# Attention and rational feed-forward on one core: output tiles take a buffer of another tag, and the transposed softmax weights are moved directly behind the transpose

## The chip, the cores and the metric

The kernel runs on one core of a Trainium2 chip, in one launch. The metric is the device time of an execution in microseconds (us). A core has several engines that each work through a queue of their own, in order, and that wait for each other by semaphores: PE (TensorE, matmuls; the loads of its stationary operand are listed as PEld), DVE (VectorE, elementwise work and reductions), ACT (ScalarE, functions and copies), POOL (GpSimd) and SP (SyncE), which here does nothing but issue transfers (DMA). Matmuls write to PSUM, whose banks are handed out to tiles like any other buffer; other tiles lie in SBUF.

## The reference

Chunked attention over 8 batches, 8 heads, 576 rows and 64 columns a head, in chunks of 64 rows, and behind it a feed-forward layer whose activation is a rational function.

```python
def _attn_ref(q, k, v):
    ...
    scores = scale * np.matmul(q_c, k_c.transpose(0, 1, 2, 4, 3))
    scores = scores - np.max(scores, axis=-1, keepdims=True)
    attn = np.exp(scores)
    attn = attn / (np.sum(attn, axis=-1, keepdims=True) + 1e-09)
    out = np.matmul(attn, v_c)
    return out.reshape(B, H, S, D).astype(np.float32)

def _moe_ref(x, w_in, w_out, a, b):
    h = x @ w_in
    h2 = h * h
    h3 = h2 * h
    P = a[0] + a[1] * h + a[2] * h2 + a[3] * h3
    Q = 1.0 + np.abs(b[0]) * np.abs(h) + np.abs(b[1]) * h2
    g = P / (Q + 1e-06)
    return (g @ w_out).astype(np.float32)

def reference(**kwargs):
    ...
    attn_out = _attn_ref(**attn_kwargs)
    B, H, S, D = attn_out.shape
    x = np.ascontiguousarray(attn_out.transpose(0, 2, 1, 3)).reshape(B * S, H * D)
    return _moe_ref(x=x, **moe_kwargs)
```

x has 4608 rows and 512 columns, `w_in` is 512x2048, `w_out` 2048x512.

## The kernel before

The 4608 rows are worked through in 18 blocks n of 256 rows (`NB`, `BT`). Each matmul of the feed-forward is done with operands split into a high and a low part (`xhi`, `xlo`, `wi_hi`, `wi_lo`, `ghi`, `glo` and so on), as three products: high by high, low by high, high by low. A block's hidden layer is cut into four steps s of 512 columns (`NST`), so a block is four steps; step g in the list `steps` is block and quarter. In a step

- `ff1` (tokens F and f, L374) makes `ph`, 48 products into a pair of PSUM banks p0 or p1, in turn from step to step;
- the chain (a, b, c, Q, I, p, J, P, g, H, R, G) makes `ghi` and `glo` of it: ACT does L378 to L398, DVE L390 to L424, with `glo` on POOL in some steps;
- `ff2` (Z, z, y, L583) adds the step two before, `LAG`, into `po`.

Beside this runs the attention of later blocks, spread over the steps. For block m = n + 1: its softmax sums and the division (n, Np) in step 0; `att_turn` (T) in step 1, a transpose on DVE within 32x32 squares, from `e` into `et` (L315); `att_move` (K), also in step 1, which sets the squares in their places by 16 transfers from `et` to `at`, issued by SP one after the other (L323); `att_av` (A) in step 3, 64 small products `psx` of `at` and `v` (L214), and behind it X and Y, which make `xhi` (ACT, L353) and `xlo` (DVE, L357), read by all `ff1` of the next block. Block n + 2 has its scores `pss`, maxima and exponentials `e` in step 3. Behind `att_av` and the scores SP loads v, q and k of the block after.

The last step of blocks 5 to 16 is not added by `ff2` but by a scheme with seven products of half size (`ff2_seven`, L540): `s_hi` and `s_lo` make `shi` and `slo` in step 0 of the next block (h, l), the products run in step 1 (V) into `xacc` and `po`, and `s_store` (w, L549 to L553) and `s_out` (o, L558) put the output tile `o` together on ACT and DVE; `put` stores it by four transfers (L600). The other blocks have `store` (L594), a copy of `po` on ACT and the same four transfers; in blocks from 3 on, it stands where V, w and o stand.

What each engine does in which order is written out by hand: `START` for the opening part up to step 12, the first of block 3, and `STEADY`, one line of tokens for each of a block's four steps, for the rest. Within an engine the order of the tokens is the order of its queue. Waits follow from the tiles: a tile is a buffer of its tag, each tag has two (`p2`) if nothing else is said, and whoever takes a buffer over waits until the last reader of the tile before is done. The tags that matter: `eo` holds `e`, `et`, `at`, `o` and, in blocks 3 and 4, `tsum`; `xhi` holds `xhi` and `shi`. In a block before the change, `eo` is given to `et` (T), then to `o` in the place of `e` (w), then to `at` in the place of `o` (K).

Of the kernel before, what the change touches and what calls it, by code (L numbers as in the profile page):

```python
# [10 lines left out]
F32 = mybir.dt.float32  # L11
# [8 lines left out]
P = 128  # L20
# [5 lines left out]
DM = 512  # L26
# [31 lines left out]
def tile_chunked_attention_rational_moe(  # L58
# [13 lines left out]
    p2 = ctx.enter_context(tc.tile_pool(name="p2", bufs=2))  # L72
# [359 lines left out]
    sums, tw, shi, slo, xacc, wide = {}, {}, {}, {}, {}, {}  # L432
# [110 lines left out]

    def s_store(n):
        x, po = xacc.pop(n), obuf.pop(n)
        wide[n] = o = p2.tile([P, 2, DM], F32, tag="eo", name=f"o{n}")
        flat = o.rearrange("p a b -> p (a b)")
        block = lambda i, k=1: flat[:, 256 * i:256 * (i + k)]
        nc.scalar.copy(block(0), x[:, 0, 0:256])  # L549
        nc.vector.tensor_add(block(1), block(0), x[:, 0, 256:512])  # L550
        nc.vector.tensor_add(block(2), block(1), x[:, 1, 0:256])
        nc.vector.tensor_add(block(3), block(2), x[:, 1, 256:512])
        nc.vector.tensor_add(block(1), block(1), x[:, 1, 256:512])  # L553
        obuf["late", n] = po
# [35 lines left out]
        return out[n * BT:(n + 1) * BT, :].rearrange("(u c t) f -> c u t f", u=UPB, c=2)  # L590

    def store(n):
        o = p2.tile([P, 2, DM], F32, tag="eo", name=f"o{n}")
        nc.scalar.copy(o, obuf.pop(n))  # L594
        put(n, o)

    def put(n, o):
        for c in range(2):
            for u in range(UPB):
                nc.sync.dma_start(out=rows_out(n)[c, u], in_=o[64 * u:64 * u + 64, c, :])  # L600
# [42 lines left out]
    def qk(n, u=None):  # L643
# [10 lines left out]
        "S": att_s, "M": att_max, "U": att_sub, "E": att_exp, "n": att_rs, "N": att_norm,  # L654
        "T": att_t, "K": att_copy, "A": att_av, "X": att_xhi, "Y": att_xlo,
        "O": store,
    }
    for k, letter in enumerate("Ff"):
# [10 lines left out]
    def run(program, then=""):  # L669
# [14 lines left out]
    one = lambda names, k: run(" ".join(f"{x}{k}" for x in names.split()))  # L684
    STEADY = (
# [4 lines left out]
    )  # L690
# [1 line left out]
    def step(g):  # L692
# [8 lines left out]
        of_early = {"S": lambda k: (att_s(k), load_qk(k + 1)), "M": att_max, "U": att_sub,  # L701
                    "E0": lambda k: att_exp_half(k, 0), "E1": lambda k: att_exp_half(k, 1)}
        of_prev = {"s": s_sums, "h": s_hi, "l": s_lo, "lp": lambda k: s_lo(k, nc.gpsimd), "w": s_store, "o": s_out}
        other = {"Q": chain_nq, "I": chain_nln, "g": chain_t, "H": chain_inv, "R": chain_g, "G": chain_split, "Gp": chain_split}
        tokens = STEADY[s].split()
        for token in tokens:
# [17 lines left out]
            elif name in of_prev:  # L724
                if fast:
                    of_prev[name](n - 1)
            elif name == "V":
                if fast:
                    ff2_seven(n - 1)
                    run(f"y{g - LAG - 1}", "F")  # L730
                else:
                    run(" ".join(f"{x}{g - LAG}" for x in "Zzy"), "F")
                    store(n - 1)
            elif name in "Zzy":
                if not (s == 0 and fast and name == "y"):
                    last = "z" if s == 0 and fast else "y"
                    run(f"{name}{g - LAG}", "F" if name == last else "z")
            elif late and s == 0 and fast and name in other:
                other[name](*steps[k])
            elif late and s == 0 and fast and name in ("L", "Lp"):  # L740
                chain_rest(*steps[k], nc.gpsimd if name == "Lp" else None)
            elif name in ("L", "Lp"):
                pass
            elif not late and s == 3 and whole and name in other:
                other[name](*steps[k])
            elif late and g == FIRST:
                pass
            elif name == "Gp" and (g == FIRST or n == NB - 1):
                run(f"G{g}")
            else:  # L750
                run(f"{name}{k}")
# [45 lines left out]
```

## Time and profile before

| | |
|---|---|
| Time, median of 3 runs | 881.47 us (879.83 to 885.39) |
| The profiled execution: its own time | 880.04 us |
| Its span, from first to last instruction | 878.2 us |
| Around the span | 1.84 us |
| Granted clock of PE, mean over the span | 0.997 |
| Moved by the transfers | 63.26 MB, mean 72 GB/s |

The page and the other views are of that one profiled execution. Busy time counts the instructions of an engine, not its waits; an instruction's row gives its start, its length in us and, in brackets, the idle time before it with what ended it. A matmul's end is modelled, and matmuls overlap: each is listed as longer than the distance to the next. `L374 PE MATMUL ph<-xhi,wi_hi` means line 374, engine PE, from `xhi` and `wi_hi` into `ph`. SPq is the queue of SP, whose instructions issue transfers. Blocks 3 to 17, the part in the order of `STEADY`, take three quarters of the span.

### The profile page before, as it was taken

What the parts mean: (1) busy time and instruction counts of PE and PEld (TensorE: products, weight loads), DVE (VectorE), ACT (ScalarE), POOL (GpSimd) and SP (SyncE); (2) the same over time, 40 slices, a digit from 0 to 9 for tenths busy, and PEclk for the clock granted to TensorE, in tenths of its full rate; (3) what the DMA queues carried; (4) which work ended last, traced back from release to release, by engine and by line L of the source; (5) the groups of instructions that cost most, each with busy time, mean ns of one, the idle gap of its engine ahead of it and who ended that gap; (6) DMA issues with size and microseconds to landing.
All of it is one profiled execution on the core that took longest, in us unless ns stands there. A gap on an engine that the chain in (4) does not pass through costs nothing.

```text
span 878.2 us, 21405 instructions
## 1 busy us (share of the span) xinstructions
PE 850.5 (97%) x9200; PEld 836.9 (95%) x9200; DVE 766.2 (87%) x753; ACT 564.3 (64%) x958; POOL 134.2 (15%) x64
## 2 busy tenths in 40 slices
PE   5999999999999999999999999999999999999998
PEld 3899999999999999999999999999999999999997
DVE  6999998997888888889899898989888888898886
ACT  5999865755647665658574757575666657584553
POOL 1222222001313111110201111111111111102000
PEclk9999999999999999999999999999999999999999
DMA  8653204012121203030211212121212030201010
GB/s 317 258 217 138 104 25 145 26 43 80 34 89 26 97 18 103 2 90 33 52 70 49 73 44 80 37 85 32 92 25 97 14 108 2 73 2 49 1 25 25
DMA packets 27263, 63.26 MB, mean 72 GB/s; under 512 B 6176, under 2 KB 13344, under 8 KB 25120
## 3 DMA queue, kind: packets, MB, share of 16 engines
q1 hardware_dynamic: 27008, 61.63, 21.8%
q8 instruction: 72, 1.18, 0.5%
q10 hardware_dynamic: 160, 0.26, 0.1%
q14 instruction: 23, 0.19, 0.1%
HBM read 45.09 MB, written 9.44 MB: 62 GB/s over the span
## 4 chain that ended last, share of the span: by engine, by line
PE 62%; SPq 18%; DMA 9%; DVE 5%; ACT 3%; issue 3%; DVEq 0%; ACTq 0%
PE ph L374 24%; PE po L583 24%; SPq L323 15%; PE xacc L540 4%; DMA out<-o 4%; DMA at<-et 3%; PE po L540 3%; SPq L600 3%; PE psx L214 2%; PE pss L214 2%; DVE o L558 2%; DMA raw<-in_w_in 1%; ACT e L298 1%; DMA v<-in_vP 1%; PE pe L583 1%
## 5 line engine op out<-in xcount | busy, mean ns | idle before, releaser
L374 PE MATMUL ph<-xhi,wi_hi 128*128 128x256 f32 x1152 | 320.8, 278 | 0.3 <-ACT xhi L353 0.3
L374 PE MATMUL ph<-xlo,wi_hi 128*128 128x256 f32 x1152 | 319.1, 277 | 1.2 <-DVE xlo L357 0.9
L374 PE MATMUL ph<-xhi,wi_lo 128*128 128x256 f32 x1152 | 318.8, 277 | 0.0
L374 PEld LDWEIGHTS ph<-xlo,wi_hi 128*128 128x128 f32 x1152 | 216.8, 188 | 1.2 <-DVE xlo L357 1.1
L374 PEld LDWEIGHTS ph<-xhi,wi_hi 128*128 128x128 f32 x1152 | 216.2, 188 | 1.6 <-ACT xhi L353 0.9
L374 PEld LDWEIGHTS ph<-xhi,wi_lo 128*128 128x128 f32 x1152 | 216.5, 188 | 0.3 <-issue 0.3
L583 PE MATMUL po<-wo_hi,ghi 128*128 128x256 f32 (+2 forms) x920 | 182.7, 280 | 0.0
L583 PE MATMUL po<-wo_lo,ghi 128*128 128x256 f32 (+2 forms) x920 | 180.9, 278 | 0.0
L424 POOL TENSOR_TENSOR glo<-B,A 128x1024 fp32r<-128x1024 f32 x36 | 88.7, 2465 | 437.7 <-DVE B L419 325.0
L394 ACT ACTIVATE A<-B,cst 128x1024 f32<-128x1024 f32 x60 | 69.4, 1156 | 121.8 <-DVE B L390 116.7
L583 PEld LDWEIGHTS po<-wo_hi,ghi 128*128 128x128 f32 x920 | 139.8, 189 | 0.9
L583 PEld LDWEIGHTS po<-wo_lo,ghi 128*128 128x128 f32 x920 | 139.8, 189 | 0.0
L378 ACT ACTIVATE A<-ph,ab 128x1024 f32<-128x1024 f32 x72 | 81.7, 1135 | 82.9 <-PE ph L374 79.6
L583 PE MATMUL po<-wo_hi,glo 128*128 128x256 f32 (+2 forms) x920 | 115.2, 277 | 0.0
L583 PEld LDWEIGHTS po<-wo_hi,glo 128*128 128x128 f32 x920 | 109.4, 188 | 0.2
L406 DVE SCALAR_TENSOR_TENSOR C<-C,ab,ph 128x1024 f32<-128x1024 f32 x72 | 92.2, 1281 | 3.1 <-ACT B L382 0.7
L386 ACT ACTIVATE C<-ph,ab 128x1024 f32<-128x1024 f32 x72 | 88.5, 1230 | 10.0 <-PE ph L374 10.0
L390 DVE SCALAR_TENSOR_TENSOR B<-B,ab,A 128x1024 f32<-128x1024 f32 x60 | 82.2, 1371 | 10.4 <-POOL glo L424 5.3
L402 DVE TENSOR_TENSOR C<-C,ph 128x1024 f32<-128x1024 f32 x72 | 86.7, 1204 | 0.4 <-ACT A L378 0.3
L398 ACT ACTIVATE A<-A,cst 128x1024 f32<-128x1024 f32 x72 | 83.1, 1155 | 2.2
L411 DVE SCALAR_TENSOR_TENSOR ghi<-C,ab,A 128x1024 fp32r<-128x1024 f32 x60 | 77.0, 1284 | 8.4 <-ACT A L398 2.0
L419 DVE SCALAR_TENSOR_TENSOR B<-C,ab,B 128x1024 f32<-128x1024 f32 x60 | 77.1, 1284 | 1.9
(140 smaller groups left out, 1150.2 us busy)
## 6 DMA issues: line engine op xcount, KB each, us to landing
v<-in_vP SPq DMA_DIRECT2D x18, 512.0 KB, 4.2
out<-o SPq DMA_DIRECT2D x68, 128.0 KB, 2.4
raw<-in_w_in SPq DMA_DIRECT2D x8, 1024.0 KB, 6.3
raw<-in_w_out SPq DMA_DIRECT2D x8, 1024.0 KB, 4.9
qk<-in_qT SPq DMA_DIRECT2D x16, 512.0 KB, 5.2
qk<-in_kT SPq DMA_DIRECT2D x16, 512.0 KB, 6.0
at<-et SPq DMA_DIRECT2D x224, 32.0 KB, 1.9
Aqk<-in_qT SPq DMA_DIRECT2D x2, 256.0 KB, 4.5
```

The lines of the kernel that those rows point to most:

```text
L323: nc.sync.dma_start(out=at[32 * j:32 * j + 32, i, :, :], in_=t[32 * i:32 * i + 32, j, :, :])
L374: nc.tensor.matmul(ph[:, fi, :], w[:, cc, f], x[:, cc, :], start=(k == 0), stop=(k == len(mm) - 1))
L378: nc.scalar.activation(ch[n, s][1], ch[n, s][0], AF.Abs, scale=b0)
L386: nc.scalar.activation(ch[n, s][3], ch[n, s][0], AF.Identity, bias=a2, scale=a3)
L390: nc.vector.scalar_tensor_tensor(B, B, b1a, A, ALU.mult, ALU.add)
L398: nc.scalar.activation(A, A, AF.Exp, bias=cst[:, 1:2], scale=-1.0)
L402: nc.vector.tensor_mul(C, C, h)
L406: nc.vector.scalar_tensor_tensor(C, C, a1, h, ALU.add, ALU.mult)
L411: nc.vector.scalar_tensor_tensor(gbuf[n, s][0], C, a0, A, ALU.add, ALU.mult)
L419: nc.vector.scalar_tensor_tensor(B, C, a0, B, ALU.add, ALU.subtract)
L424: (engine or nc.vector).tensor_mul(gbuf[n, s][1], B, A)
L583: nc.tensor.matmul(accs[n][i][:, cols], g[:, fi, i * 128:(i + 1) * 128], w[:, FPS * s + fi, cols], start=start, stop=stop,)
```

## The change

Three things. The output tile of `s_store` takes a buffer of the tag `xhi` instead of `eo`; so does that of `store` for blocks from 2 on. And in step 1, the token K stands directly behind T, ahead of V, w and o, where it stood behind these.

```diff
     def s_store(n):
         x, po = xacc.pop(n), obuf.pop(n)
-        wide[n] = o = p2.tile([P, 2, DM], F32, tag="eo", name=f"o{n}")
+        wide[n] = o = p2.tile([P, 2, DM], F32, tag="xhi", name=f"o{n}")
...
     def store(n):
-        o = p2.tile([P, 2, DM], F32, tag="eo", name=f"o{n}")
+        o = p2.tile([P, 2, DM], F32, tag="xhi" if n > 1 else "eo", name=f"o{n}")
         nc.scalar.copy(o, obuf.pop(n))
         put(n, o)
...
-        "F f a b c T V w o K Q I p J P g H R G",
+        "F f a b c T K V w o Q I p J P g H R G",
```

With it `eo` is given to `et` (T) and to `at` in the place of `e` (K); `o` takes, of the two buffers of `xhi`, the one that holds no live `xhi`: in the blocks with seven products that of `shi`, and the next block's `xhi` then follows `o` in it.

The order on SP, steps 1 to 3 of three blocks, before; numbers behind the names are those of the tiles.

```order
L600 DMA out<-o_3377 64x512 x4
L323 DMA at_3383<-et_3327 32x256 x16
L123 DMA v_3608<-in_vP 128x1024
L117 DMA qk<-in_qT 128x1024
L117 DMA qk<-in_kT 128x1024
L600 DMA out<-o_3960 64x512 x4
L323 DMA at_3971<-et_3899 32x256 x16
L123 DMA v_4196<-in_vP 128x1024
```

The same place of SP's queue after the change:

```order
L323 DMA at_3329<-et_3327 32x256 x16
L600 DMA out<-o_3394 64x512 x4
L123 DMA v_3608<-in_vP 128x1024
L117 DMA qk<-in_qT 128x1024
L117 DMA qk<-in_kT 128x1024
L323 DMA at_3901<-et_3899 32x256 x16
L600 DMA out<-o_3977 64x512 x4
L123 DMA v_4196<-in_vP 128x1024
```

The 16 transfers of `at` have changed places with the four stores of `o`; nothing else moved on SP. On the other engines no instruction changes its place. What they wait for does change; on ACT, the first copy into `o` in step 1, with the semaphores that it waits for (those of the DMA queues begin with DMAHW):

```order
 L382 ACTIVATE B_1_3895<-ph_1_3844 128x1024
 L386 ACTIVATE C_1_3897<-ph_1_3844,ab 128x1024
-L549 COPY o_3960<-xacc_3901 128x256 [waits DVE_49,PE_49]
+L549 COPY o_3977<-xacc_3918 128x256 [waits PE_49]
 L394 ACTIVATE A_1_3893<-B_1_3895,cst 128x1024 [waits DVE_49,Activation_49]
 L398 ACTIVATE A_1_3893<-A_1_3893,cst 128x1024 [waits Activation_49]
```

The copy no longer waits for DVE, whose transpose read the buffer's last tile `e`. In step 3 of the same block, again on ACT, the cast into `xhi`:

```order
 L382 ACTIVATE B_3_4235<-ph_3_4114 128x1024
-L353 CAST xhi_4237<-psx_4163 128x2x4x128 [waits PE_49]
+L353 CAST xhi_4237<-psx_4163 128x2x4x128 [waits DMAHW4_49,DMAHW3_49,DMAHW5_49,DMAHW2_49,PE_49]
 L386 ACTIVATE C_3_4241<-ph_3_4114,ab 128x1024
 L478 ACTIVATE A_3_4233<-B_3_4235,cst 128x1024 [waits DVE_49,Activation_49]
```

The cast, in its old place, now also waits for four transfers, the stores of `o`.

## The prediction

> **What bounds the kernel now.** I read the page first, then the waits of PE, then the order of time around one of these waits on PE, SP, DVE and ACT.
>
> The page: busy time of each engine and its share of the span.
> ```profile
> span 878.2 us, 21405 instructions
> PE 850.5 (97%) x9200; PEld 836.9 (95%) x9200; DVE 766.2 (87%) x753; ACT 564.3 (64%) x958; POOL 134.2 (15%) x64
> ```
> PE is the bound, so only what PE idles through, or runs at a lower clock, can be won. The waits of PE and of its weight loads from 180 to 820 us (engine, line, releaser: total, times, longest) are these alone:
> ```profile
> PE psx L214 <- DMA at<-et: 11.8, 17, 1.2
> PEld psx L214 <- issue: 8.9, 12, 1.3
> PEld psx L214 <- DMA at<-et: 4.9, 6, 0.9
> ```
> In the steady part PE waits for one thing: the moved softmax weights `at`, which the products `psx` read. SP's own waits hold the row that says why `at` is late: the 16 transfers of L323 stand behind the four output stores in SP's queue, and must also wait until those have landed, because `at` takes the buffer of `o`.
> ```profile
> SPq L323 <- DMA out<-o: 24.0, 27, 1.8
> ```
> One block in order of time (start, length, what, idle before it), first DVE and ACT, then SP, then PE; here `et` is the transposed tile, `o` the output tile:
> ```profile
> 367.82 1.24 DVE L315 STREAM_TRANSPOSE et<-e 128x1024 f32<-128x1024 f32 x1
> 369.14 0.37 ACT L549 COPY o<-xacc 128x256 f32<-128x256 f32 x1 [0.78 <-DVE et L315]
> 371.81 1.22 DVE L558 TENSOR_TENSOR o<-o,po 128x1024 f32<-128x1024 f32 x1 [0.60 <-PE po L583]
> 384.27 1.28 DVE L406 SCALAR_TENSOR_TENSOR C<-C,ab,ph 128x1024 f32<-128x1024 f32 x1
> 389.23 1.02 ACT L382 ACTIVATE B<-ph 128x1024 f32<-128x1024 f32 x1
> 390.94 1.01 ACT L353 CAST xhi<-psx 128x1024 fp32r<-128x1024 f32 x1 [0.69 <-PE psx L214]
> 391.99 1.23 DVE L357 TENSOR_TENSOR xlo<-psx,xhi 128x1024 fp32r<-128x1024 f32 x1 [2.43 <-ACT xhi L353]
> ```
> ```profile
> 373.10 2.43 SPq L600 DMA_DIRECT2D out<-o  x4
> 377.44 10.75 SPq L323 DMA_DIRECT2D at<-et  x16
> ```
> ```profile
> 388.12 0.45 PE L214 MATMUL psx<-at,v 64*64 64x64 f32 x6
> 389.79 1.05 PE L214 MATMUL psx<-at,v 64*64 64x64 f32 x57 [1.23 <-DMA at<-et]
> 390.69 0.22 PE L214 MATMUL psx<-at,v 64*64 64x64 f32 x1
> ```
> `et` is ready at 369.06, but its first transfer goes out at 377.44, 8.4 us later; the issue of 16 takes 10.75 us and the last lands about when PE is already in `psx`. PE can start `psx` at 388.12 and ends at 390.91.
>
> **The change part by part.** *The move of K ahead of V, w and o, and the new buffer of `at`.* Nothing is added or removed: the same 16 transfers and 4 stores, in the other order, on SP. After it the transfers need only `et` and the buffer of `e`, both free when L315 ends. They are issued from 369.1 to 369.1 + 10.75 = 379.8. The time from issue to landing (last number, medians):
> ```profile
> out<-o SPq DMA_DIRECT2D x68, 128.0 KB, 2.4
> at<-et SPq DMA_DIRECT2D x224, 32.0 KB, 1.9
> ```
> `at` is complete at 379.8 + 1.9 = 381.7, 6.4 us before PE wants it at 388.1. The wait should go in all 14 blocks that have such a move (224 transfers by 16).
>
> What is it worth? Take the stretch from the start of the first `psx` product to the end of the last. Without a wait, in the opening part, and then the first and the last of the 14 hindered ones, with the shortest between:
> ```profile
> 109.27 1.16 PE L214 MATMUL psx<-at,v 64*64 64x64 f32 x64
> ...
> 199.52 0.52 PE L214 MATMUL psx<-at,v 64*64 64x64 f32 x6
> 201.67 0.22 PE L214 MATMUL psx<-at,v 64*64 64x64 f32 x1
> ...
> 575.33 0.39 PE L214 MATMUL psx<-at,v 64*64 64x64 f32 x6
> 576.41 1.08 PE L214 MATMUL psx<-at,v 64*64 64x64 f32 x57 [0.69 <-DMA at<-et]
> 577.34 0.22 PE L214 MATMUL psx<-at,v 64*64 64x64 f32 x1
> ...
> 808.61 0.32 PE L214 MATMUL psx<-at,v 64*64 64x64 f32 x2
> 809.69 0.53 PE L214 MATMUL psx<-at,v 64*64 64x64 f32 x4 [0.76 <-DMA at<-et]
> 810.92 1.11 PE L214 MATMUL psx<-at,v 64*64 64x64 f32 x58 [0.70 <-DMA at<-et]
> ```
> The unhindered stretch is 1.16 us; the first hindered one 2.37, the shown block 2.79, the shortest 2.23, the last 3.42. The 14 together are 37.2 us. The upper bound of the gain is 37.2 - 14 × 1.16 = 20.9 us; the lower one is the idle time that the waits name, 11.8 us. They differ because idle is counted from the modelled end of the product before, some 0.2 us after the next could have started (17 × 0.2 = 3.4), and because each of four products waits for the transfers of its quarter, which leaves smaller holes. Some of that handling stays when everything has landed. The nearest row is the shortest stretch, where one quarter alone was late: 2.23 - 0.69 - 0.2 = 1.34. I take 1.3 us a stretch: 37.2 - 14 × 1.3 = **19.0 us**, near the upper end.
>
> [...]
>
> *The clock after the last stretch.* The last block has no `pss` behind its `psx`, and the granted clock (the last but two of the numbers) fell to half there; the 48 products that follow took 7.37 us where the same ones elsewhere took 5.66 (from the chain that ended last):
> ```profile
> 811.91:815.33 3.42, 3.42 (x21) 3.37 (x16) 2.22 (x2) 2.12 (x2) 0.66 (x1) 0.50 0.00 0
> 812.03 7.37 PE po L583 x48
> 671.86 5.66 PE po L583 x48
> ```
> That is 1.7 us. It follows a stretch of 3.42 us in which PE did little; with 1.3 us of it I expect full clock, as the products at 671.86 had it behind their own block's shorter stretch. Bounds: 0 and **1.7 us**; I take 1.7.
>
> *The output tile in a buffer of `xhi`.* Two buffers carry `xhi`, `shi` and now `o`. (a) `o` takes the buffer that `shi` had. Its first copy (L549) no longer waits for L315 but for the last product that reads `shi`. PE's rows there:
> ```profile
> 366.56 2.04 PE xacc L540 x18
> 368.60 1.36 PE po L540 x12
> ```
> The first six of the twelve read `shi` and end at 368.60 + 0.68 = 369.28, with the pipeline's 0.2 at 369.5: the copy starts 0.1 to 0.4 us later than 369.14. Behind it stand ACT's Ln and DVE's L550 to L553; L558 waited 0.60 us for PE anyway, so this covers it, with PE no faster. If that cover were gone, 0.4 us in each of 11 blocks would delay DVE, not PE. Cost: 0, bounds 0 and 0.4 × 11 = 4.4. (b) The next `xhi` (L353) takes `o`'s buffer and must wait until the stores have landed. The stores now go out behind the 16 transfers, at 379.8, take 2.43 to issue and 2.4 to land: 384.7. The cast started at 390.94 and could start at 390.25, when the ACTIVATE before it ends. 5.5 us are to spare; cost 0. (c) The v load, next in SP's queue, overwrites the one tile that `psx` reads and waits for `psx` in any case; cost 0.
>
> *What is late next.* PE gains about 1.4 us a block, the cast at most 0.69 (ACT's own work comes before it), so DVE and ACT fall up to 0.8 us behind PE, 1.2 with the copy of (a). `psx` needs the bank that L406 frees at 385.55, 2.6 us before 388.12; 1.4 would be left. The next block's first ff1 products need `xlo`, done at 393.22:
> ```profile
> 391.84 5.66 PE po L583 x48
> 397.50 5.48 PE ph L374 x48
> ```
> 4.3 us to spare, 3.4 afterwards. So no new wait of PE. DVE has room too: a block lasts (808.61 - 199.52) / 13 = 46.85 us, and DVE is idle for 13% of the span, some 6 us of it.
>
> **Sum.** 19.0 + 1.7 = 20.7 us. The profiled execution took 880.04 us (span 878.2 and 1.84 around it): 859.3. Its own time is 1.4 under the median of the runs, 881.47; from that the sum gives 860.8. I take the middle, 860.0 us.
>
> **The rivals.** *Only the named waits, or less, come back: DVE and ACT become the pace.* If the lag above were not absorbed, PE would gain in each block only what the cast gains, the 7.7 us that ACT waited for `psx`:
> ```profile
> ACT xhi L353 <- PE psx L214: 7.7, 13, 1.3
> ```
> 880.04 - 7.7 - 1.7 = 870.6. Against it stand DVE's 6 idle us in a block and the 1.4 us left at the bank; for it, that this spare time is smallest exactly at `psx`. Chance 0.11.
>
> *The change doesn't do what it says:* `at` isn't earlier in effect, because the 16 transfers slow down or another wait takes the place of the store's. The issue would have to stretch from 10.75 us to over 17, or DVE's L315 to run 6.4 us later; time 880. Nothing in the rows speaks for it. Chance 0.05.
>
> *Slower: the stores now hold up `xhi`.* The cast waits for landed stores that stand behind 16 transfers. It decides from the point where the cast is so late that `xlo` passes 397.5, 3.4 us after its new time, thus when the stores land after 390.25 + 3.4 = 393.7 rather than 384.7. Each further us is one us per block, 14 in all; at 2.4 us more PE would lose 34 and win 20.7: 893. [...] Chance 0.02.
>
> **How the numbers follow.** The forecast, `psx` without its wait and no new one, has 0.80; the three rivals 0.11, 0.05 and 0.02; 0.02 is for what I don't see. The forecast's own range runs from 880.04 - 20.9 - 1.7 = 857.4, and a little for the scatter of runs, to 880.04 - 11.8 = 868.2 with no gain of clock; I give 856.5 to 869.0, which leaves out the rivals, 2 in 10. One per cent of 881.47 is 8.8 us, about what a measurement of this kernel tells from no change: under 872.7 is faster. The forecast and the first rival, with a little taken off for mixtures of both, give 0.90 for faster; the second, and those mixtures, 0.08 for the same; 0.02 slower.
>
> **What the profile of the changed kernel would show.** Right: the row of PE's waits for `at` is gone; each `psx` stretch is 1.16 to 1.4 us; SP issues L323 within 0.5 us of the end of L315 and L600 behind it; the period of a block falls from 46.8 to about 45.4; no half clock near the last `psx`; ACT's L353 waits for PE or nothing. Wrong: a wait of PE's `psx` on DVE or of ff1 on `xlo` (first rival), SP still late with L323 (second), ACT's L353 waiting for `out` (third). If the stretches shrink only by the idle time named, the step from idle to starts was wrong.

## The result and the profile after

| | before | after |
|---|---|---|
| Time, median | 881.24 us (4 runs, 879.83 to 885.39) | 857.50 us (4 runs, 855.93 to 857.81) |
| The profiled execution: time, span | 880.04, 878.2 us | 857.70, 855.6 us |

The ratio is 0.972, 95% interval 0.9685 to 0.9754: 2.8% faster. The forecast was 860.0 us, with 856.5 to 869.0 as its range.

The page of the kernel after, its busy times and the chain that ended last, by engine:

```profile
span 855.6 us, 21362 instructions
PE 839.4 (98%) x9200; PEld 828.5 (97%) x9200; DVE 765.1 (89%) x753; ACT 562.6 (66%) x958; POOL 134.3 (16%) x64
PE 96%; DMA 2%; DVE 1%; SPq 0%; issue 0%; ACT 0%
```

The chain of the kernel before, by engine:

```profile
PE 62%; SPq 18%; DMA 9%; DVE 5%; ACT 3%; issue 3%; DVEq 0%; ACTq 0%
```

PE's work is the same 9200 products. The chain that ended last ran through SP's queue and the transfers for 27% of the span; now it runs along PE itself for 96%; the row of PE's waits for `at` is gone, and between 180 and 800 us PE waits for nothing that the profile lists.

The same block as in the prediction, after (start, length, what, idle before it). First DVE and ACT:

```profile
363.26 1.24 DVE L315 STREAM_TRANSPOSE et<-e 128x1024 f32<-128x1024 f32 x1
363.80 0.37 ACT L549 COPY o<-xacc 128x256 f32<-128x256 f32 x1 [0.83 <-PE po L540]
366.41 1.22 DVE L558 TENSOR_TENSOR o<-o,po 128x1024 f32<-128x1024 f32 x1 [0.37 <-PE po L583]
383.83 1.01 ACT L382 ACTIVATE B<-ph 128x1024 f32<-128x1024 f32 x1
384.74 1.02 ACT L353 CAST xhi<-psx 128x1024 fp32r<-128x1024 f32 x1
```

SP's queue in the same block:

```profile
364.53 10.06 SPq L323 DMA_DIRECT2D at<-et  x16
374.70 2.45 SPq L600 DMA_DIRECT2D out<-o  x4
```

And PE:

```profile
382.71 1.16 PE L214 MATMUL psx<-at,v 64*64 64x64 f32 x64
```

The transfers go out 0.03 us after the end of L315 (364.50), where it took 8.4 us before. The issue ends at 374.59; the last transfer, issued from 374.00 on, lands 1.9 us after that start, at 375.9. PE begins `psx` 6.8 us later, at 382.71, and runs all 64 products in one piece. The 14 stretches from the first `psx` product to the end of the last, 37.2 us before, add up to 16.4: thirteen of 1.16 us and one of 1.33. ACT's cast (L353) now follows the ACTIVATE before it with no wait; the stores behind which it must wait were issued by 377.15, and the last of them landed at 380.2, 4.5 us before the cast starts.

So the time went like this: 37.2 - 16.4 = 20.8 us in the stretches, and 1.7 us by the half clock that followed the last stretch before and doesn't now. The 48 products behind it, 7.37 us before, from the chain of the kernel after:

```profile
790.11 1.16 PE L214 MATMUL psx<-at,v 64*64 64x64 f32 x64
791.27 5.66 PE po L583 x48
```

Together 22.5 of the 22.6 us between the spans; the opening is 0.6 us longer and the time between the stretches 0.6 us shorter, which cancels.

### The profile page after: what moved, and what is told of

It reads as the page before. It is cut to its first block, busy times and chain, and to the rows that moved or that the text cites. A ratio compares the mean times of both kernels' runs of the same rounds, so it can differ in the third digit from the quotient of the medians.

```text
span 855.6 us, 21362 instructions
## 1 busy us (share of the span) xinstructions
PE 839.4 (98%) x9200; PEld 828.5 (97%) x9200; DVE 765.1 (89%) x753; ACT 562.6 (66%) x958; POOL 134.3 (16%) x64
## 4 chain that ended last, share of the span: by engine, by line
PE 96%; DMA 2%; DVE 1%; SPq 0%; issue 0%; ACT 0%
PE ph L374 46%; PE po L583 37%; PE xacc L540 4%; PE po L540 3%; PE psx L214 2%; PE pss L214 2%; PE pe L583 1%; DMA v<-in_vP 1%; DMA raw<-in_w_in 1%; PE pl L193 1%; PE po L611 0%; PE pe L611 0%; PE pst L310 0%; DVE raw L175 0%; DVE raw L162 0%; DVE sm L278 0%
```

## The experiments

**Which half of the change matters?** The first two kernels do one part alone. The buffer alone:

```diff
-        "F f a b c T K V w o Q I p J P g H R G",
+        "F f a b c T V w o K Q I p J P g H R G",
```

> The output tile takes a buffer of the tag xhi, as in the changed kernel; K keeps its old place behind V, w and o. Theory (the wait for the landed stores was the harm, not the order): in the changed kernel's trace L558 ends at 367.63; four stores take 2.45, sixteen transfers 10.06, the last lands 1.8 later, at 381.9, against 382.71 when PE wants it. No wait of psx, 857.5 us, give or take 1.5. Rival (the place in SP's queue is needed too): psx still waits some 0.3 to 0.7 us in each of 14 blocks, 862 to 868 us.

Measured: 858.81 us, ratio 0.9747 (0.9723 to 0.9771). One block of it, SP, DVE and PE:

```profile
414.55 2.61 SPq L600 DMA_DIRECT2D out<-o  x4
417.26 10.78 SPq L323 DMA_DIRECT2D at<-et  x16
```
```profile
413.25 1.22 DVE L558 TENSOR_TENSOR o<-o,po 128x1024 f32<-128x1024 f32 x1 [0.54 <-PE po L583]
```
```profile
384.02 1.36 PE L214 MATMUL psx<-at,v 64*64 64x64 f32 x63
...
429.55 1.16 PE L214 MATMUL psx<-at,v 64*64 64x64 f32 x64
```

SP stores as soon as `o` is there (414.47) and goes on with `at` without waiting for the landing, which is what the buffer gives. The issue ends at 428.04; by the 1.8 to 1.9 us from issue to landing, the medians before and after, `at` lands at some 429.3, just before PE wants it at 429.55: eleven stretches are 1.16 us, the three others 1.22 to 1.43 (the block at 384.02 is one), 16.8 us in all against 16.4. The theory holds: the buffer alone brings nearly all of the gain. The place of K ahead of the stores is worth 0.4 us of stretches here; what it brings is the time to spare, 6.8 us in the blocks of the middle instead of some 0.3 in this one.

The order alone:

```diff
-        wide[n] = o = p2.tile([P, 2, DM], F32, tag="xhi", name=f"o{n}")
+        wide[n] = o = p2.tile([P, 2, DM], F32, tag="eo", name=f"o{n}")
...
-        o = p2.tile([P, 2, DM], F32, tag="xhi" if n > 1 else "eo", name=f"o{n}")
+        o = p2.tile([P, 2, DM], F32, tag="eo", name=f"o{n}")
```

> K directly behind T, as in the changed kernel; the output tile stays in the tag eo, where it now follows et. Theory: ACT's first copy into o (L549, L594) waits until the sixteen transfers have read et, 10.1 + 1.8 = 11.9 us after the end of L315, instead of some 0.3; po comes free that much later, PE waits for it at the ff2 of step 2, 7 to 10 us in each of 14 blocks: 955 to 1000 us. Rival (at is early, and the rest is hidden): 857 to 865 us.

Measured: 1005.55 us, ratio 1.1412 (1.1384 to 1.1440). PE's waits between 180 and 900 us, the wait of ACT's first copy between 180 and 800, then DVE in one block, then the granted clock (0.50, the last but two of the numbers) in the stretch of time behind:

```profile
PE po L583 <- DVE o L558: 77.6, 10, 8.1
PE po L583 <- ACT o L594: 24.5, 3, 9.2
```
```profile
ACT o L549 <- DMA at<-et: 105.7, 8, 13.5
```
```profile
406.63 1.24 DVE L315 STREAM_TRANSPOSE et<-e 128x1024 f32<-128x1024 f32 x1
419.79 0.42 DVE L550 TENSOR_TENSOR o<-o,xacc 128x256 f32<-128x256 f32 x1 [11.92 <-ACT o L549]
```
```profile
419.42:426.25 6.83, 3.42 (x16) 3.42 (x17) 6.25 (x8) 2.48 (x3) 0.00 (x0) 0.50 0.29 68
```

`psx` is never late here, yet the kernel is 14% slower than before: `o` follows `et`, so its first copy waits until all transfers have read `et`, DVE stands for 11.92 us behind it and PE for some 8 us for `po`. The place and the size of the wait were as expected; the time lies 5 us above the expected range, because the clock fell where PE stood, which the expectation did not have in it: half for 6.83 us in this block, and 0.942 in the mean over the span of 1004.0 us, where the changed kernel had 1.000. The named waits alone, 77.6 + 24.5 = 102.1 us, would give some 960 us; the half clock, by that mean 2 × 0.058 × 1004 = 116 us of it, can have cost up to half of that, 58 us (before, 3.42 us of it cost 1.7), where 46 remain.

**How much time is to spare?** Two kernels that cut `at` into more transfers. Halving the first eight, then all sixteen:

```diff
-                nc.sync.dma_start(out=at[32 * j:32 * j + 32, i, :, :], in_=t[32 * i:32 * i + 32, j, :, :])
+                for h in ((slice(0, 4), slice(4, 8)) if j < 2 else (slice(0, 8),)):
+                    nc.sync.dma_start(out=at[32 * j:32 * j + 32, i, h, :], in_=t[32 * i:32 * i + 32, j, h, :])
```

> The changed kernel with at moved by 24 transfers: the first eight are halved. It prices the time to spare. Theory: issue takes 24 x 0.63 = 15.1 us, at lands 1.2 us before psx; the stores land 15.1 + 2.45 + 2.4 = 20.0 us after the end of L315, and with cast, xlo and DVE's work up to the next L315 the loop is some 45.0 us, just under the period of 45.27: 857.5 us, give or take 2. Rival (issuing costs more than it shows, or the spare time is less than 5 us): over 862 us.

Measured: 862.49 us, ratio 0.9790 (0.9759 to 0.9821). PE's waits, then a block at the start of the steady part and one in its middle (L315 on DVE, `psx` on PE):

```profile
PE psx L214 <- DMA at<-et: 2.8, 4, 1.0
```
```profile
231.26 1.24 DVE L315 STREAM_TRANSPOSE et<-e 128x1024 f32<-128x1024 f32 x1
...
413.08 1.24 DVE L315 STREAM_TRANSPOSE et<-e 128x1024 f32<-128x1024 f32 x1
```
```profile
247.79 0.33 PE L214 MATMUL psx<-at,v 64*64 64x64 f32 x2
249.86 1.05 PE L214 MATMUL psx<-at,v 64*64 64x64 f32 x57 [0.98 <-DMA at<-et]
...
432.53 1.16 PE L214 MATMUL psx<-at,v 64*64 64x64 f32 x64
```

A miss by 3 us, on the side of the rival. In the middle the expectation held: the stretches are 1.16 us. The first three are 2.1 to 3.2 us long, since in the second of them, shown here, PE wants `psx` 15.3 us after the end of L315 (247.79 - 232.50), not 18.2 (432.53 - 414.32); in the others it is 16.9 and 16.0. In the second and third, DVE has the work on `tsum` before L315, a likely reason that wasn't tested; the first has none, and its reason stays open. The last stretch, 1.73 us, is late too, by the author's estimate for a transfer that landed late: in the changed kernel the transfers of `at` land in 1.8 us in the median, but in up to 3.3. The prediction's 6.4 us to spare was read from one block and isn't true of all 14.

> The changed kernel with at moved by 32 transfers of half size. Issue takes 20.1 us, at lands 3.8 us after PE wants it, and the stores land 25 us after the end of L315. Theory (the third rival of the prediction exists as a mechanism and decides beyond some 5 us of spare time): the cast into xhi waits for the stores, and the loop L315, transfers, stores, cast, xlo, DVE's work to the next L315 is 1.2 + 20.1 + 4.9 + 1.0 + 22.7 = 50.0 us a block against 45.27: 857.5 + 14 x 4.7 = 923 us, 905 to 930. Rival (only the late at counts, the stores are hidden): 2 to 3.6 us a block, 885 to 908 us, and ACT's cast waits for psx alone.

Measured: 910.71 us, ratio 1.0346 (1.0316 to 1.0377). One block on SP and ACT:

```profile
434.10 20.97 SPq L324 DMA_DIRECT2D at<-et  x32
455.18 2.45 SPq L601 DMA_DIRECT2D out<-o  x4
```
```profile
457.07 1.01 ACT L354 CAST xhi<-psx 128x1024 fp32r<-128x1024 f32 x1 [1.83 <-PE psx L214]
```

The number falls into the theory's range, but not for its reason: the cast starts at 457.07, while the issue of the stores goes on to 457.63 (455.18 + 2.45) and the last of them lands at 460.5. It waits for `psx` alone (32.5 us in 13 waits of ACT's), as the rival said, whose range, 885 to 908 us, is missed by 3 us. With 32 transfers the allocation of buffers had come out otherwise: all `xhi` in one of the two, `shi` and `o` in the other (with 24 as well, where the fourth store, issued from 250.39 on (248.57 + 1.82), lands by the median of 2.4 us at some 252.8, `psx` ends at 250.98 (250.76 + 0.22), and ACT's waits name no store). The wait that this run was to price wasn't in it. What it does price is a late `at`: 4 us of stretch in most blocks, over 6 in the first three, 63.5 us in all, and half clock behind some of them: the mean clock is 0.988 over the span of 909.0 us. The next run names the buffers, so that each `xhi` follows `o` as in the changed kernel.

```diff
+    def xt(n):
+        return "xhi_a" if n == 0 or n > 2 and n % 2 else "xhi_b"
...
-        shi[n] = p2.tile([P, 4, 2, 128], F32R, tag="xhi", name=f"shi{n}")
+        shi[n] = p2.tile([P, 4, 2, 128], F32R, tag=xt(n), bufs=1, name=f"shi{n}")
...
-        wide[n] = o = p2.tile([P, 2, DM], F32, tag="xhi", name=f"o{n}")
+        wide[n] = o = p2.tile([P, 2, DM], F32, tag=xt(n), bufs=1, name=f"o{n}")
```

> As the kernel with 32 transfers, but with the buffers named one by one, so that each xhi follows the output tile as in the changed kernel; with 32 transfers the allocation had put all xhi into one buffer and shi and o into the other, so that run never had this wait. Theory (third rival's mechanism): there the last store landed at 460.5, and the cast began at 457.1; now it must wait, 3.4 us a block, of which up to 1.3 us is covered by DVE's waits: 910.7 + 13 x 2.3 to 3.4 = 940 to 955 us, and ACT's L354 waits for out. Rival (the wait is hidden): 908 to 914 us.

Measured: 951.80 us, ratio 1.0779 (1.0758 to 1.0800), some 40 us more than with the other buffers. ACT's waits, then one block on ACT and SP:

```profile
ACT xhi L357 <- DMA out<-o: 92.6, 12, 9.6
```
```profile
423.76 1.02 ACT L357 CAST xhi<-psx 128x1024 fp32r<-128x1024 f32 x1 [8.03 <-DMA out<-o]
```
```profile
417.87 2.46 SPq L604 DMA_DIRECT2D out<-o  x4
```

The cast now does wait for the stores, as the prediction's third rival had it: that mechanism exists, and is hidden in the changed kernel only by the time to spare: 4.0 to 5.8 us in the later blocks, but 3.0, 1.6 and 1.7 us in the first three of the 14 (in the second, the last store lands at 246.52 and the cast starts at 248.08).

**Is it free in the changed kernel?** All `xhi` but those of blocks 1 and 2 in one buffer, `shi` and `o` in another, with the 16 transfers of the changed kernel:

```diff
-        wide[n] = o = p2.tile([P, 2, DM], F32, tag="xhi", name=f"o{n}")
+        wide[n] = o = p2.tile([P, 2, DM], F32, tag="xo", bufs=1, name=f"o{n}")
...
-        shi[n] = p2.tile([P, 4, 2, 128], F32R, tag="xhi", name=f"shi{n}")
+        shi[n] = p2.tile([P, 4, 2, 128], F32R, tag="xo", bufs=1, name=f"shi{n}")
```

> The changed kernel with 16 transfers, but all xhi in one buffer and shi and o in the other, so that the cast into xhi waits for no store; shi waits for it instead, in the next block. Theory (the cast's new wait costs nothing in the changed kernel, as 5 us are to spare): 857.5 us, give or take 1.5, and the same stretches of 1.16 us. Rival (the wait for four more semaphores costs something): 1 us or more below 857.5.

Measured: 857.79 us, ratio 0.9723 (0.9697 to 0.9748), with 0.9720 for the changed kernel: the cast's wait for the stores costs nothing that can be measured. The stretches are 1.16 us, as in this one (the profiled execution itself took 862.04 us; its excess lies in the opening part, since the first of the 14 stretches starts 4.4 us later than in the changed kernel):

```profile
387.14 1.16 PE L214 MATMUL psx<-at,v 64*64 64x64 f32 x64
```

**Does the half clock come of the held-up last stretch?** The old buffer and order in one block alone:

```diff
+        if n == 16 and s == 1:
+            tokens = "F f a b c T V w o K Q I p J P g H R G".split()
...
-        wide[n] = o = p2.tile([P, 2, DM], F32, tag="xhi", name=f"o{n}")
+        wide[n] = o = p2.tile([P, 2, DM], F32, tag="eo" if n == 15 else "xhi", name=f"o{n}")
```

> The changed kernel, but in block 16 alone the output tile is in eo and K stands behind o, as before: only the psx of the last block (17), which has no pss behind it, is held up. Theory (the half clock at the end of the kernel before came of that stretch): the stretch grows from 1.16 to 3.4 us, the granted clock falls to half for 3.4 us, the 48 products behind it take 7.4 us instead of 5.66: span 855.6 + 2.2 + 1.7 = 859.5 us. Rival (the clock fell for another reason, such as the time run so far): the stretch grows alone, span 857.8.

Measured: 859.58 us, span 858.6. PE at the last stretch, and the 48 products behind it:

```profile
791.35 0.32 PE L214 MATMUL psx<-at,v 64*64 64x64 f32 x2
791.97 0.62 PE L214 MATMUL psx<-at,v 64*64 64x64 f32 x4 [0.29 <-DMA at<-et]
793.18 1.11 PE L214 MATMUL psx<-at,v 64*64 64x64 f32 x58 [0.60 <-DMA at<-et]
```
```profile
794.30 5.67 PE po L583 x48
```

The stretch is 2.95 us and no half clock follows (1.00 from 794.78 to 798.19): a held-up last stretch alone does not bring it, and the theory fails in that form. The span, 3.0 us up, is 1.8 of stretch and 1.2 of a later start of the steady part. The same edit one place earlier, 12 for 16 and 11 for 15:

> The same, but in block 12 instead of 16: only the psx of block 13 is held up, with pss behind it. Both theories: the stretch grows from 1.16 to some 2.6 us, the clock stays at full, span 855.6 + 1.4 = 857.0 us. A half clock here would say that a held-up psx alone brings it, and not the missing pss.

Measured: 860.76 us, span 859.8, 4.2 us up. The stretch grew to 3.19 us, 0.6 more than expected, and the steady part began 1.9 later; the clock stayed full (1.00 from 611.79 to 618.60). The times of these two kernels and of the one with its own buffers were taken beside the same runs of before, 883.42 us: against the 857.79 of the latter, one held-up block costs 1.8 and 3.0 us. The stretches account for 1.8 and 2.0 of these; the start of the steady part alone differs by up to 1.9 us between the traces of these two and of the changed kernel.

What tells the cases apart, as far as the traces show it, is where the stretch lies. In the kernel before, half clock lasts 3.41 us, from 811.91 to 815.33, and the next change of the clock comes 61.4 us later, 18 times as long; with 32 transfers a half clock lasts 3.42 us (505.27 to 508.69), with the order alone 6.83. It followed some of the pieces of 3.41 us in which PE did little. Rows of four such pieces (PE busy and number of products are the first two numbers behind the length): the kernel before, the one with the old order in block 16, and, of the kernel with 32 transfers, one that was followed by half clock and one that was not.

```profile
808.50:811.91 3.41, 1.95 (x66) 1.57 (x64) 1.51 (x2) 2.03 (x2) 1.69 (x1) 1.00 0.11 30
```
```profile
791.37:794.78 3.41, 2.49 (x69) 2.10 (x69) 1.72 (x2) 2.48 (x3) 1.48 (x1) 1.00 0.08 22
```
```profile
501.86:505.27 3.41, 1.17 (x69) 1.20 (x73) 0.72 (x1) 1.42 (x2) 2.35 (x1) 1.00 0.23 55
...
454.07:457.49 3.42, 1.70 (x105) 1.73 (x109) 0.48 (x1) 1.59 (x3) 2.35 (x1) 1.00 0.35 83
```

The stretch of the kernel before, 808.61 to 812.03, fills its piece; the other, 791.35 to 794.30, leaves 0.5 us of full-size products at the end of its own. Busy time alone does not order the pieces: 1.95 us was followed by half clock, 1.70 us in the last row was not. So that the place of the stretch decides is read from these traces; no run moved the same stretch against the pieces, and what of PE's work in a piece decides stays open.

## Why the prediction was right

- *What bounds the kernel*, PE, and its one wait, `at`: right. With the wait gone PE needed nothing else; the time between two stretches in the blocks of the middle is 44.1 us before and after.
- *The move*: `at` at 6.4 us to spare was about right in the blocks of the middle (375.9 against 382.71, 6.8 us); the prediction counted the 1.9 us to landing from the end of the last issue, the view from its start. In the first three blocks it is 5.2, 2.6 and 2.8 us: the run with 24 transfers showed that these differ.
- *Both causes of the late `at`* were put together, the place behind the stores and the wait for their landing. The single parts show that they are far apart: the buffer alone gives 0.9747, the order alone 1.1412.
- *The size*: 1.3 us for a free stretch was too much, it is 1.16, the value of the opening part, and the upper bound of the gain, 20.9 us, was hit (20.8 against 19.0). So nothing of the handling of the four waits stays on PE when all transfers have landed; why it is hidden wasn't tried. The waits' named idle time, 11.8 us, was little more than half of the gain, and the idle time of the weight loads, 8.9 + 4.9 = 13.8, two thirds of the 20.8 gained: the step from idle time to start times was right.
- *The clock*: 1.7 us, as in the sum, but as a property of that execution, and so in part luck. A kernel with the same hold-up in its last block didn't show the half clock, and two of the recorded executions of the kernel before had a mean clock of 1.000 over the span, which leaves no room for one: 3.42 us at half make the mean 0.998 (882.02 and 882.47 us, not faster than the others).
- *The output tile in a buffer of `xhi`*: (a) the copy L549 waits for PE (0.83 us), its delay is covered, L558 still waits 0.37 us for PE; (b) 4.5 us to spare in the shown block where the prediction had 5.5, but only 1.6 in the tightest, and free by the run with own buffers.
- *What is late next*: L315 stands 19.45 us ahead of `psx` where it was 20.30: DVE has fallen 0.85 us behind PE, as reckoned (0.8), and no wait of PE came of it. So the first rival fell; the second fell with SP's rows; the third is real as a mechanism, some 40 us with 32 transfers, and doesn't bite with 16.

The forecast is 2.5 us above the median. From the profiled execution alone it would have been 859.3 against 857.7, and these 1.6 us are the 1.8 by which the stretches were mis-sized, less 0.2 of the smaller differences.

## What to carry to other kernels

A tile that is read late and written early should not follow, in its buffer, a tile whose last reader is a store: the wait for the landing goes into the loop of the whole block (before, 24.0 us of SP's waits; with 32 transfers, 92.6 us of ACT's), though the two have nothing to do with each other. Before an order is changed, ask which buffers the new order will chain: the same move was worth 0.4 us of stretches here with the right buffers, and cost 14% with the wrong ones. And read the time to spare in every block, not in one: here it was 6.8 us in most and 2.6 in the tightest. The price of a stall, last, is the distance of start times against the same work where it runs free, not the idle time that a view of waits names: 20.8 us here against 11.8.

## What the runs showed of the hardware

- PE's clock cost more than expected where PE stood: with 8 us of waiting a block (the order alone), half clock followed, 6.83 us in the block shown and some 116 us in all by the mean clock of 0.942, while of the 14 hindered stretches of the kernel before, 2.2 to 3.4 us long, one alone was followed by half clock (0.50 from 811.91 to 815.33), the one that filled one of the pieces of 3.41 us.
- A transfer's issue on SP cost about the same for half the bytes: 32 transfers of 16 KB took 20.97 us, 16 of 32 KB 10.06, so 0.63 to 0.66 us each. Cutting this move in two lengthened its issue 2.08 times.
- How the buffers of a tag were handed out changed with the number of transfers: the same lines of code gave two allocations with 16 and with 24 or 32 transfers, and with them another wait of the cast. With 32, ACT waited for no store; with the buffers named, 92.6 us. A run that is to price a wait must name its buffers.
